# Windowed attention, forward and backward: loading four quads ahead, with one more buffer for x and one less for the turned tokens

## The chip, the cores and the metric

The kernel runs on one core of a Trainium2 chip. The metric is the device time of one execution in microseconds; the figure for a kernel is the median of several runs. One execution of the kernel before was also recorded by the hardware profiler, with every instruction, every semaphore update and every DMA packet. The names used: PE or TensorE (matrix products), DVE or VectorE, ACT or ScalarE, POOL or GpSimd, SP or SyncE, which here only issues DMAs.

## The reference

The input x is an image of 256 x 256 tokens with 384 channels in bfloat16. It is cut into windows of 8 x 8 tokens, attention with one head of 384 channels is computed within each window, and the result is projected. The kernel returns the output and the gradients of x, of `wqkv` and of `wo` for a given gradient of the output.

```python
xw = x cut into 1024 windows of 64 tokens
qkv = xw @ wqkv
q, k, v = (qkv[..., :C], qkv[..., C:2 * C], qkv[..., 2 * C:])
scale = C ** (-0.5)
p = _softmax(jnp.einsum('bqc,bkc->bqk', q, k) * scale, axis=-1)
o = jnp.einsum('bqk,bkc->bqc', p, v) @ wo
_out, _vjp = jax.vjp(_f, x, wqkv, wo)
_grads = _vjp(grad_out)
```

## The kernel before

**Tiling.** Two windows, 128 tokens, fill the 128 partitions; four such pairs make a quad of eight windows. There are 128 quads. Per quad the kernel loads x as the tile `xq` and the gradient of the output as `dq`, each 128 x 4 x 384 in bfloat16, in four DMAs of 96 KB each.

**Weights.** The weights are multiplied together once at the start (`A_sb` from the query and key weights with the scale, `B_sb` from the value weights and `wo`, and their transposes), so that each quad needs fewer products.

**Stages of a quad.** The main loop (L495) runs steps i from 0 to 128, and step i works on three quads at once:

- *quad i+1*: `project` (L173) forms two products with the turned gradient `dT` (kind 0) and the turned x `xT` (kind 1); ScalarE casts them into `yz`, and `gather` (L187) copies them on VectorE into `zy`.
- *quad i*: `scores` (L198), the softmax in six parts (`soft`, L210), and `uv` (L250), whose PSUM banks ScalarE casts into `uq` and `vq`; then `turn` (L260) turns the small probability matrices, on VectorE or, for the first three quads and the last, by a DMA (`crossed`).
- *quad i-1*: `attend` (L283), in four slots: products with `dq`, `xq`, the turned tokens `tok`, `uq` and `vq`; ScalarE and VectorE take the PSUM banks out as `Wq`, `Uq`, `o` and `d`, and GpSimd stores `o` and `d` to memory.

Beside this, each group of `GQ` = 3 finished quads is multiplied into the weight gradients (`gf_rows`, `gf_halves`), two of six products in each step. A quad's `xq` therefore lives until its group is done.

**Turns.** SyncE issues three DMA transposes a quad: `dT` and `xT` from `dq` and `xq` in `load_turn` (L153), called in step i for quad i+2, and `tok` from `zy` in `to_tokens` (L193), called in step i for quad i. `dT` has two buffers, `xT` three, `tok` three.

**Loads.** `load` (L141) is called within step i for quad i + `AHEAD`. It puts four gradient loads on GpSimd's queue (L145), and two x loads on SyncE's (L147); `load_rest` (L149) puts the other two x loads on ScalarE's queue (L151), behind the casts of `yz` and ahead of the casts of `attend`. Ahead of the loop the loads of quads 0, 1 and 2 are issued.

**Order.** Every engine's order is the order of the calls (`manual_schedule`). So SyncE's queue in step i is: `dT` and `xT` of quad i+2, `tok` of quad i, then the two x loads; in the first steps a turn of `cr` into `PS` stands ahead of the x loads. Each engine works its queue in order. The wait of an instruction for its data, for the buffer that it overwrites and for its DMA completion counter is put in by the framework. The counters for DMAs from SyncE and ScalarE are `DMAHW0` to `DMAHW7`, taken in rotation in the order in which the program has the DMAs, and a DMA that takes one waits for the last DMA that used it.

Of the kernel before, what the change touches and what calls it, by code (L numbers as in the profile page):

```python
# [11 lines left out]
BF16 = mybir.dt.bfloat16  # L12
F32 = mybir.dt.float32

P = 128
WIN = 8
WT = WIN * WIN
QUAD = 4
# [5 lines left out]
def kernel(  # L24
# [22 lines left out]
    _, H, W, C = x.shape  # L47
    CK = C // P
# [5 lines left out]
    grp = ctx.enter_context(tc.tile_pool(name="grp", bufs=2 * GQ + 1))  # L54
    qp = ctx.enter_context(tc.tile_pool(name="qp", bufs=2))
# [26 lines left out]
    def fetch_rest():  # L82
        nc.sync.dma_start(out=w_sb[:, :, columns(0)], in_=w_in[:, :, columns(0)])
        nc.scalar.dma_start(out=w_sb[:, :, columns(1)], in_=w_in[:, :, columns(1)])
# [32 lines left out]
    def weight_rest():  # L117
        turn_blocks(B_sb, BT_sb)
        turn_blocks(AT_sb, A_sb)

    def windows(ap, st, first, count=2):
        row, col = st["at"]
        return ap[0, row + WIN * first:row + WIN * (first + count), col:col + WIN, :]
# [2 lines left out]
    OTHER = {0: HI, WT: LO}  # L126

    def load_first(st):
        st["xq"] = xq = grp.tile([P, QUAD, C], BF16, tag="xq", name="xq", bufs=2 * GQ + 4)
        st["dq"] = dq = qp.tile([P, QUAD, C], BF16, tag="dq", name="dq", bufs=6)  # L130
        for t in range(QUAD):
            (nc.sync, nc.scalar)[t % 2].dma_start(out=dq[:, t, :], in_=windows(grad_out, st, 2 * t))
        fetch_rest()
        for t in range(2):
            nc.sync.dma_start(out=xq[:, t, :], in_=windows(x, st, 2 * t))
        nc.gpsimd.tensor_copy(out=spare[:, 0:1], in_=dq[:, QUAD - 1, 0:1])
        for t in range(2, QUAD):
            nc.gpsimd.dma_start(out=xq[:, t, :], in_=windows(x, st, 2 * t))
        nc.gpsimd.tensor_copy(out=spare[:, 1:2], in_=xq[:, 1, 0:1])

    def load(st, on_act=0):  # L141
        st["xq"] = xq = grp.tile([P, QUAD, C], BF16, tag="xq", name="xq", bufs=2 * GQ + 4)
        st["dq"] = dq = qp.tile([P, QUAD, C], BF16, tag="dq", name="dq", bufs=6)
        for t in range(QUAD):
            nc.gpsimd.dma_start(out=dq[:, t, :], in_=windows(grad_out, st, 2 * t))  # L145
        for t in range(QUAD - on_act):
            nc.sync.dma_start(out=xq[:, t, :], in_=windows(x, st, 2 * t))  # L147

    def load_rest(st, on_act):  # L149
        for t in range(QUAD - on_act, QUAD):  # L150
            nc.scalar.dma_start(out=st["xq"][:, t, :], in_=windows(x, st, 2 * t))  # L151
# [39 lines left out]
        nc.vector.tensor_copy(out=st["zy"][:, kind, :, :, :, :], in_=src)  # L191

    def to_tokens(st):  # L193
        st["tok"] = tok = qp.tile([P, 2, CK, QUAD, P], BF16, tag="tok", name="tok", bufs=3)
        nc.sync.dma_start_transpose(out=tok[:].rearrange("p b m t k -> p (b m t) k"),
                                    in_=st["zy"][:].rearrange("p b m t s k -> p (b m t s k)"))

# [177 lines left out]
    def step(c, b, a, ahead):  # L375


        def on(st):
            return (lambda f, *r: f(st, *r)) if st is not None else (lambda f, *r: None)
        C_, B, A = on(c), on(b), on(a)  # L380
        if b is not None and c is None:
            weight_rest()
        B(scores)
        B(soft, 0)
        B(uv, 0, 0)
        B(uv, 0, 1)
        B(soft, 1)
        B(uv, 1, 0)
        B(uv, 1, 1)
        B(soft, 2)  # L390
        B(soft, 3)
        B(uv, 2, 0)
        B(uv, 2, 1)
        B(uv, 3, 0)
        B(uv, 3, 1)
        B(soft, 4)
        for mo in range(CK):
            A(project, 0, mo)
        B(soft, 5)
        B(turn)  # L400
        if ahead is not None:
            load(ahead, ON_ACT)
        A(gather, 0)
        for mo in range(CK):
            A(project, 1, mo)
        if ahead is not None:
            load_rest(ahead, ON_ACT)
        for rows in range(1 if a is not None else 2):
            if fill:
                gf_rows(*fill.pop(0))  # L410
        slots = attention(c) if c is not None else iter(())
        for t in range(QUAD):
            if t == 2:
                A(gather, 1)
            next(slots, None)
        for rest in slots:
            pass
# [4 lines left out]
    quads = [(row, col) for col in range(0, W, WIN) for row in range(0, H, 2 * WIN * QUAD)]  # L422
    n = len(quads)
    sts = [{"at": q, "i": i, "crossed": i < GQ or i == n - 1} for i, q in enumerate(quads)]
    AHEAD = 3
    dw_out = out_2.rearrange("(m p) j -> p m j", p=P)
    dwo_out = out_3.rearrange("(m p) n -> p m n", p=P)

    def weight_gradients(group):
        def product_row(k, out, left, right, sc):  # L430
            pe = ring.tile([P, C], F32, tag="r", name="pe")
            for m in range(CK):
                nc.tensor.matmul(pe[:], lhsT=left[:, m, k * P:(k + 1) * P], rhs=right[:, m, :],  # L433
                                 start=(m == 0), stop=(m == CK - 1))
            if sc is not None and k % 2:
                nc.scalar.activation(out=out, in_=pe[:], func=ACT.Copy, scale=sc)
            elif sc is not None:
                nc.vector.tensor_scalar(out=out, in0=pe[:], scalar1=sc, scalar2=None, op0=ALU.mult)
            else:
                copy_out(k, out, pe[:])  # L440

        def rows(name):
            return grp.tile([P, CK, C], BF16, tag="xq", name=name, bufs=2 * GQ + 4)

        GFT = [grp.tile([P, CK, C], BF16, tag="Wq", name="GFT") for f in range(2)]
        for i in range(CK + 1):
            next(group)
        turn_blocks(GFT[0], final[0])
        for i in range(CK - 1):
            next(group)  # L450
        for part, left, right in ((0, GFT[0], w_sb[:, :, columns(1)]), (1, final[0], w_sb[:, :, columns(0)])):
            dw = rows("dw")
            for k in range(CK):
                product_row(k, dw[:, k, :], left, right, scale)
            nc.sync.dma_start(out=dw_out[:, :, columns(part)], in_=dw[:])
        turn_blocks(GFT[1], final[1])
        dwo = rows("dwo")
        for k in range(CK):
            product_row(k, dwo[:, k, :], w_sb[:, :, columns(2)], final[1], None)
        nc.sync.dma_start(out=dwo_out, in_=dwo[:])  # L460
        dw = rows("dw")
        for k in range(CK):
            product_row(k, dw[:, k, :], GFT[1], woT_sb, None)
            (nc.sync, nc.scalar)[k % 2].dma_start(out=dw_out[:, k, columns(2)], in_=dw[:, k, :])

    with tc.manual_schedule(engines=MANUAL):
        spare = sm.tile([P, 3], BF16, name="spare", bufs=1)
        fetch_weights()
        warm_up(7)
        nc.scalar.copy(out=spare[:, 2:3], in_=B_sb[:, 0, 0:1])  # L470
        make_identity(nc, ident[:])
        nc.gpsimd.memset(GF_acc[:], 0.0)
        load_first(sts[0])
        load(sts[1])
        load(sts[2])
        load_turn(sts[0])
        load_turn(sts[1])
        turn_blocks(wT[2], w_sb, 2 * CK)
        weight_product(BT_sb, wo_sb, wT[2], None)
        turn_on_pe(sts[0], "dq", "dT")  # L480
        for mo in range(CK):
            project(sts[0], 0, mo)
        turn_blocks(wT[0], w_sb, 0)
        turn_blocks(wT[1], w_sb, CK)
        weight_product(A_sb, wT[0], wT[1], scale)
        turn_on_pe(sts[0], "xq", "xT")
        gather(sts[0], 0)
        for mo in range(CK):
            project(sts[0], 1, mo)
        gather(sts[0], 1)  # L490
        turn_on_pe(sts[1], "dq", "dT")
        held = []
        last = None
        get = lambda i: sts[i] if 0 <= i < n else None
        for i in range(n + 1):  # L495
            if 0 <= i < n - 2:
                load_turn(sts[i + 2])
            if 0 <= i < n:
                to_tokens(sts[i])
            step(get(i - 1), get(i), get(i + 1), get(i + AHEAD))  # L500
            if i == 1:
                turn_blocks(woT_sb, wo_sb)
            if i > 0:
                held.append(sts[i - 1])
                sts[i - 1] = None
            if held and i == n:
                last = gf_final(held)
            elif len(held) == GQ:
                fill.extend((held, f, ma) for f in range(2) for ma in range(CK))
                held = []  # L510
        while fill:
            gf_rows(*fill.pop(0))
        weight_gradients(last)
# [30 lines left out]
```

## Time and profile before

| what | value |
|---|---|
| runs | 1904.77, 1904.13 and 1914.19 us |
| median of the runs | 1904.77 us |
| profiled execution, its own time | 1904.35 us |
| its span, first to last instruction | 1902.6 us |
| TensorE clock granted | 1.00 |
| VectorE, ScalarE, GpSimd busy | 88%, 80%, 45% |
| time the packets of SyncE's, GpSimd's and ScalarE's queues took, as shares of 16 DMA engines | 77.8%, 32.0%, 6.2% |
| tok turn, issue to landing | 10.1 us in the median |
| xT turn, issue to landing | 7.6 us |
| dT turn, issue to landing | 7.1 us |
| x load on SyncE and on ScalarE, issue to landing | 4.9 and 6.0 us |
| gradient load on GpSimd, issue to landing | 5.8 us |

How to read it: a line of a group gives the source line, the engine, the operation and the tiles. Lines with SPq or ACTq are DMA issues by the sequencer of SyncE or ScalarE; the time on such a line is that of the issue, and the landing comes later. A wait shown with "<-" names what ended it, as far as semaphore events tell. The shares of the three queues are sums over packets that overlap, so they may add up to more than 100%.

SyncE's queue in time, two steps from the middle of the span (start, length of the issue, what):

```
802.39 1.44 SPq L158 DMA_TRANSPOSE dT<-dq  x1
804.32 3.49 SPq L158 DMA_TRANSPOSE xT<-xq  x1
807.91 5.27 SPq L195 DMA_TRANSPOSE tok<-zy  x1
813.24 1.24 SPq L147 DMA_DIRECT2D xq<-in_x_dram  x2
814.65 2.07 SPq L158 DMA_TRANSPOSE dT<-dq  x1
819.78 1.90 SPq L158 DMA_TRANSPOSE xT<-xq  x1
821.78 4.95 SPq L195 DMA_TRANSPOSE tok<-zy  x1
826.83 1.19 SPq L147 DMA_DIRECT2D xq<-in_x_dram  x2
```

### The profile page before, as it was taken

What the parts mean: (1) busy time and instruction counts of PE and PEld (TensorE: products, weight loads), DVE (VectorE), ACT (ScalarE), POOL (GpSimd) and SP (SyncE); (2) the same over time, 40 slices, a digit from 0 to 9 for tenths busy, and PEclk for the clock granted to TensorE, in tenths of its full rate; (3) what the DMA queues carried; (4) which work ended last, traced back from release to release, by engine and by line L of the source; (5) the groups of instructions that cost most, each with busy time, mean ns of one, the idle gap of its engine ahead of it and who ended that gap; (6) DMA issues with size and microseconds to landing.
All of it is one profiled execution on the core that took longest, in us unless ns stands there. A gap on an engine that the chain in (4) does not pass through costs nothing.

```text
span 1902.6 us, 57253 instructions
## 1 busy us (share of the span) xinstructions
PE 1889.1 (99%) x22333; PEld 1125.4 (59%) x22333; DVE 1668.2 (88%) x3616; ACT 1527.2 (80%) x3354; POOL 859.7 (45%) x1575
## 2 busy tenths in 40 slices
PE   8999999999999999999999999999999999999999
PEld 5565566556655665566556655665565556556655
DVE  5888888888888888888888888888888888888887
ACT  7888878887878788878888887888788878887885
POOL 4444445444444444444444444444444445444432
PEclk9999999999999999999999999999999999999999
DMA  9999999999999999999999999999999999999994
GB/s 206 231 219 227 209 207 226 231 205 222 219 220 216 210 215 228 201 222 223 222 226 198 227 213 220 227 206 216 219 223 225 219 215 215 216 224 221 199 212 104
DMA packets 948913, 408.22 MB, mean 215 GB/s; under 512 B 830689, under 2 KB 924097, under 8 KB 948641
## 3 DMA queue, kind: packets, MB, share of 16 engines
q1 hardware_dynamic: 836224, 228.16, 77.8%
q0 software_dynamic: 75168, 150.91, 32.0%
q10 hardware_dynamic: 37248, 25.48, 6.2%
q8 instruction: 175, 2.87, 0.7%
q14 instruction: 98, 0.79, 0.2%
HBM read 101.84 MB, written 101.84 MB: 107 GB/s over the span
## 4 chain that ended last, share of the span: by engine, by line
PE 96%; DMA 2%; ACT 1%; ACTq 0%; DVE 0%; issue 0%
PE pj L169 51%; PE pg L169 13%; PE ph L353 13%; PE sd L169 5%; PE pw L298 5%; PE po L298 4%; PE pu L298 4%; DMA dT<-dq 2%; PE pd L298 1%; ACTq L151 0%; PE pe L433 0%; ACT yz L185 0%; DMA dq<-in_grad_out_dram 0%; DMA w_sb<-in_wqkv_dram 0%; PE pt L103 0%
## 5 line engine op out<-in xcount | busy, mean ns | idle before, releaser
L318 POOL DMA_DIRECT2D out_dram<-o x512 | 274.0, 535 | 790.7 <-ACT o L302 781.0
L309 ACT CAST Wq<-pw 128x384 bf16<-128x384 f32 x506 | 243.8, 482 | 281.1 <-PE pw L298 270.9
L169 PEld LDWEIGHTS <-xT 128*128 128x128 bf16 x3072 | 291.8, 98 | 182.7 <-issue 0.6
L145 POOL DMA_DIRECT2D dq<-in_grad_out_dram x508 | 268.4, 535 | 184.6 <-PE pj L169 85.6
L169 PE MATMUL pj<-B_sb,xT 128*128 128x384 bf16 x1536 | 333.6, 326 | 0.3 <-issue 0.3
L169 PE MATMUL pj<-AT_sb,xT 128*128 128x384 bf16 x1536 | 333.3, 326 | 0.0
L312 DVE CAST Uq<-pu 128x384 bf16<-128x384 f32 x512 | 282.8, 552 | 16.3 <-PE pu L298 4.1
L320 POOL DMA_DIRECT2D out_dram<-d x480 | 276.6, 576 | 19.9 <-DVE GF_acc L335 5.2
L169 PE MATMUL pj<-xT,A_sb 128*128 128x512 bf16 x1152 | 269.5, 379 | 0.7 <-ACT xT L95 0.7
L169 PE MATMUL pj<-dT,BT_sb 128*128 128x512 bf16 x1152 | 269.5, 379 | 0.6 <-ACT dT L95 0.6
L298 PE MATMUL pd<-tok,ps 64*64 64x384 bf16 x2048 | 256.4, 326 | 3.1 <-ACT o L302 1.7
L183 ACT CAST yz<-pj 128x512 bf16<-128x512 f32 x384 | 225.1, 586 | 38.0 <-PE pj L169 29.3
L302 ACT CAST o<-po 128x384 bf16<-128x384 f32 x512 | 249.6, 488 | 4.4 <-PE po L298 2.7
L258 ACT CAST vq<-pj 128x384 bf16<-128x384 f32 x512 | 247.0, 482 | 3.2
L258 ACT CAST uq<-pj 128x384 bf16<-128x384 f32 x512 | 244.3, 477 | 4.5 <-PE pj L169 2.8
L185 ACT CAST yz<-pj 128x512 bf16<-128x512 f32 x384 | 224.5, 586 | 23.9 <-PE pj L169 0.9
L273 DVE STREAM_TRANSPOSE PS<-ps 32x256 bf16<-32x256 bf16 x496 | 216.2, 436 | 9.5
L169 PEld LDWEIGHTS <-xq 128*128 128x128 bf16 x1572 | 153.6, 98 | 115.2 <-issue 0.9
L353 PEld LDWEIGHTS <-xq 64*64 64x64 bf16 x6000 | 176.3, 107 | 67.3
L353 PE MATMUL ph<-Wq,xq 64*64 64x384 bf16 x3984 | 204.3, 322 | 0.0
L169 PEld LDWEIGHTS <-A_sb 128*128 128x128 bf16 x1152 | 112.7, 98 | 136.4 <-ACT xT L95 0.5
L169 PEld LDWEIGHTS <-BT_sb 128*128 128x128 bf16 x1152 | 112.7, 98 | 122.8 <-DVE dT L97 0.4
(96 smaller groups left out, 3055.4 us busy)
## 6 DMA issues: line engine op xcount, KB each, us to landing
out_dram<-o POOLq DMA_DIRECT2D x512, 96.0 KB, 5.1
dq<-in_grad_out_dram POOLq DMA_DIRECT2D x508, 96.0 KB, 5.8
out_dram<-d POOLq DMA_DIRECT2D x480, 96.0 KB, 5.5
xq<-in_x_dram SPq DMA_DIRECT2D x260, 96.0 KB, 4.9
xq<-in_x_dram ACTq DMA_DIRECT2D x250, 96.0 KB, 6.0
out_dram<-d POOLq DMA_DIRECT2D x64, 48.0 KB, 5.3
tok<-zy SPq DMA_TRANSPOSE x128, 10.1
xT<-xq SPq DMA_TRANSPOSE x127, 7.6
```

The source lines that it names most:

```text
L145: nc.gpsimd.dma_start(out=dq[:, t, :], in_=windows(grad_out, st, 2 * t))
L169: nc.tensor.matmul(out, lhsT=lhsT, rhs=rhs, start=start, stop=stop)
L183: ENG[EV["z"][mo]](out=yz[:, mo, :, 0:4:3, :], in_=pj[:])
L185: ENG[EV["y"][mo]](out=yz[:, mo, :, 1:3, :], in_=pj[:])
L258: cp(out=dst[:, t, :], in_=pj[:])
L298: nc.tensor.matmul(dst[o, :], lhsT=operand(st, lhs, t, h), rhs=operand(st, rhs, t, h), **flags)
L302: copies[EV[name][i]](out=sb[rows, :], in_=src[rows, :])
L309: copies[EV["W"][t] if st["i"] >= GQ else "DA"[t % 2]](out=st["Wq"][:, t, :], in_=pw[:])
L312: copies[EV["U"][t]](out=st["Uq"][:, t, :], in_=pu[:])
L318: nc.gpsimd.dma_start(out=windows(out_0, st, 2 * t), in_=o)
L320: nc.gpsimd.dma_start(out=windows(out_1, st, 2 * t - 1), in_=d if t else above[:])
L353: nc.tensor.matmul(dst[o, :], lhsT=st["xq"][h, t, ma * P + o.start:ma * P + o.stop], rhs=st["UW"[f] + "q"][h, t, :], start=(i == 0), stop= ...
```

## The change

`AHEAD` goes from 3 to 4, so `load` and `load_rest` in step i are for quad i+4. Step 0 gets one call more: `load` of quad 3, with all four of its x loads on SyncE, right behind `tok` of quad 0. The tag `xq` has 11 buffers in place of 10 (3,072 bytes a partition each), and `tok` has two in place of three (6,144 bytes a partition each). `dq` keeps its six buffers.

```diff
@@ load_first, load, rows of weight_gradients
-grp.tile([P, QUAD, C], BF16, tag="xq", name="xq", bufs=2 * GQ + 4)
+grp.tile([P, QUAD, C], BF16, tag="xq", name="xq", bufs=2 * GQ + 5)
@@ to_tokens
-        st["tok"] = tok = qp.tile([P, 2, CK, QUAD, P], BF16, tag="tok", name="tok", bufs=3)
+        st["tok"] = tok = qp.tile([P, 2, CK, QUAD, P], BF16, tag="tok", name="tok", bufs=2)
@@
-    AHEAD = 3
+    AHEAD = 4
@@ the main loop
             if 0 <= i < n:
                 to_tokens(sts[i])
+            if i == 0:
+                load(sts[AHEAD - 1])
             step(get(i - 1), get(i), get(i + 1), get(i + AHEAD))
```

More of the change, by code (lines that the diff above doesn't have):

```diff
@@ L128, in load_first @@
     def load_first(st):
-        st["xq"] = xq = grp.tile([P, QUAD, C], BF16, tag="xq", name="xq", bufs=2 * GQ + 4)
+        st["xq"] = xq = grp.tile([P, QUAD, C], BF16, tag="xq", name="xq", bufs=2 * GQ + 5)
         st["dq"] = dq = qp.tile([P, QUAD, C], BF16, tag="dq", name="dq", bufs=6)
@@ L141, in load @@
     def load(st, on_act=0):
-        st["xq"] = xq = grp.tile([P, QUAD, C], BF16, tag="xq", name="xq", bufs=2 * GQ + 4)
+        st["xq"] = xq = grp.tile([P, QUAD, C], BF16, tag="xq", name="xq", bufs=2 * GQ + 5)
         st["dq"] = dq = qp.tile([P, QUAD, C], BF16, tag="dq", name="dq", bufs=6)
@@ L442, in rows @@
         def rows(name):
-            return grp.tile([P, CK, C], BF16, tag="xq", name=name, bufs=2 * GQ + 4)
+            return grp.tile([P, CK, C], BF16, tag="xq", name=name, bufs=2 * GQ + 5)
         GFT = [grp.tile([P, CK, C], BF16, tag="Wq", name="GFT") for f in range(2)]
```

## The prediction

> **What bounds the kernel now.** I read the page first (engines, slices, queues), then TensorE's waits, then the chain of waits, then SyncE's order in time, and last the waits that the built program holds.
>
> The page and its view of stages, in order. Columns of the third line: stretch, length, then busy time and instructions of PE, PEld, DVE, ACT, POOL; granted clock, share of 16 DMA engines, GB/s.
>
> ```profile
> span 1902.6 us, 57253 instructions
> PE 1889.1 (99%) x22333; PEld 1125.4 (59%) x22333; DVE 1668.2 (88%) x3616; ACT 1527.2 (80%) x3354; POOL 859.7 (45%) x1575
> 69.50:1863.40 1793.90, 1792.22 (x21379) 1069.28 (x21376) 1592.30 (x3443) 1456.38 (x3197) 820.28 (x1500) 1.00 1.19 217
> ```
>
> TensorE is busy in 1792.22 of the 1793.90 us between quad 4's start and the last quad's, at clock 1.00. Modelled ends could hide stalls, so I check the pace in the chain of waits (start, length, what), where one piece marks each quad:
>
> ```profile
> 69.51 7.79 PE pj L169 x42
> 84.08 7.79 PE pj L169 x42
> 98.64 7.79 PE pj L169 x42
> ...
> 521.04 7.79 PE pj L169 x42
> 551.56 7.79 PE pj L169 x42
> 566.12 7.79 PE pj L169 x42
> ```
>
> A quad costs 14.57 us, almost without variation: (521.04 - 69.51) / 31 = 14.566. The step 521.04 to 551.56 is two quads, 29.13, plus 1.39 us of stall. Counted from one step's first score matmul to the next (step i works quad i's scores), just four steps after the start are long: 1.38 (step 36), 1.02 (54, of it 0.34 TensorE's own "issue"), 0.15 (94) and 0.65 us (123): 3.2 us in all. The chain around the first names the cause:
>
> ```profile
> 537.66 7.55 DMA dT<-dq
> 545.21 0.02 issue
> 545.23 0.55 ACTq L151
> 545.78 0.04 issue
> 545.82 1.35 ACTq L151
> 547.17 0.04 issue
> 547.21 0.49 ACT Wq L309
> ```
>
> ScalarE's queue is in order. Its first x load (L151) started 0.02 us after a turn of the gradient landed, and the evictions of the attention stood behind it; TensorE then lacked a PSUM bank (idle 0.98 us). The load does not need that turn. It waits because hardware DMAs (SyncE's and ScalarE's) take completion counters in rotation, eight of them, with seven such DMAs a quad: each waits for the one eight earlier. In the program of before, ScalarE's first load of step i waits for dT of quad i+2. Normally it starts at 8.70 us into the step; wherever it started later than 8.80 us, from step 19 on, that start is dT's landing plus 0.02. A step stalls once the second load's issue ends past about 11.05 us (step 36: end 12.43, stall 1.38).
>
> **The change, part by part.**
>
> *Loads a quad earlier.* Quad 3's second half moves from ScalarE (250 x loads to 248) to SyncE (260 to 262); GpSimd keeps its 508. Nothing is added in sum. What moves is SyncE's waiting. Before:
>
> ```profile
> SPq L158 <- DMA xq<-in_x_dram: 185.3, 146, 3.6
> SPq L158 <- DMA dq<-in_grad_out_dram: 86.2, 51, 5.4
> ```
>
> Those 185.3 + 86.2 us, 2.1 a quad, vanish, as x and gradient landed a step ago. SyncE's medians are 2.1 (dT), 2.5 (xT), 5.7 (tok) and 2 x 0.6 (x), 11.5 us a quad. So the queue can gain some 3 us a quad on TensorE until another wait holds it. TensorE gains nothing from that directly: the least margin from a turn's landing to its first use, from step 5 on, was 9.6 (dT), 6.9 (xT) and 4.5 us (tok).
>
> *One buffer less for tok.* SyncE's tok turn of quad i now waits for the last attention product of quad i-2, which ends about 0.1 us before step i begins (813.79 and 813.89 in the trace). So far it mostly started 4 to 6 us into the step, so that wait is over already unless SyncE gets ahead; then it pins tok at 0 us. Behind it stand the x pair, dT and xT of quad i+3. dT also waits for the projection that frees its old buffer, at 6.7 us. So: tok at 0 to 5.7, x pair to 7, dT to 9.1, xT to 11.7, landing by 17 (7.6 us after issue). They are used over 10 us later, so the new wait costs 0; without that cover a late tok would stop TensorE by its whole delay.
>
> *The counters rotate differently.* In the new program ScalarE's first load waits for **xT** of quad i+2, not dT. At the old phase that would be bad (xT landed at 10.6 us in the median, up to 14.6). At the pinned phase xT lands at about 17 - 14.6 = 2.4 us, 6 us ahead of 8.70. The stalls from late dT go: 1.38 + 0.68 + 0.15 + 0.65 = -2.9 us (bounds -2.9 and 0).
>
> *GpSimd.* Its gradient loads stand at the same place in its queue. The new buffer wait (attention of quad i-2) is met before the output stores ahead of it have gone out: 0.
>
> *The start.* Step 0 now issues four more x loads on SyncE, behind tok of quad 0 (issue ends at 27.84), each 0.6 us; the turn PS of quad 0, first behind them, goes from 27.95 to about 30.4 and lands 3.4 us later, 33.8, before its use at 37.13. But ScalarE's second load of step 0 now waits for the **second** of those four, issued at 28.5. Such a load lands in 4.9 us by the median row; a pair issued at 29.21 landed at 33.5, 4.3 us after its first. So ScalarE is held until 32.8, plus 0.6 for the issue. The next in its queue:
>
> ```profile
> 28.20 0.61 ACTq L151 DMA_DIRECT2D xq<-in_x_dram  x1
> 29.94 0.48 ACT L258 CAST uq<-pj 128x384 bf16<-128x384 f32 x1 [1.40 <-PE pj L169]
> ```
>
> That cast goes from 29.94 to 33.4: 3.4 us late, and TensorE, which soon has no free bank, with it. Bounds: 0 (banks cover it) and 5. I take 3.4, since ScalarE is the busier side there (TensorE waits for its casts at 38.96). Against it: in step 3 ScalarE's second load waited for dT (issued 56.15, 8.83 us to landing), and TensorE idled 1.28 us; dT comes earlier there, -1.3 (bounds -1.9 and 0).
>
> Sum: +3.4 - 2.9 - 1.3 = **-0.8 us**, on the profiled execution's 1904.35 (span 1902.6): 1903.6. The median of the runs lies 0.4 above that execution, so **1904 us**. The bounds give -4.8 to +5.0: 1900 to 1910. About 0.5%, 9.5 us, is what a measurement here tells from no change.
>
> **The rivals.**
>
> *1. Slower: ScalarE's issues beside back-to-back turns.* Pinned, dT and xT go out at 7 to 11.7 in every step, just around the two loads from 8.70. So far these met tok's issue, and the second took 0.55 to 1.51 us. If both take 1.51 the second ends at 8.70 + 1.51 + 0.04 + 1.51 = 11.76, 0.71 past 11.05: 0.71 x 120 = 85 us, 1989. It decides only from an end past 11.05; a tenth of a microsecond past gives 12 us, 1916. For it: the repeated phase. Against: the first took 0.55 even beside tok, and the sum of the longest seen, 8.70 + 0.55 + 0.04 + 1.51, is 10.80. Chance 0.13.
>
> *2. Slower: SyncE does not get ahead.* The queues' packets take 77.8 + 32.0 + 6.2% of 16 engines; if the DMA engines rather than waits set SyncE's pace, xT lands at 10.6 us as before, and ScalarE's first load waits for it: second ends at 10.6 + 0.55 + 0.04 + 0.65 = 11.84, 0.8 us past: 0.8 x 120 = 96 us, 2001. For it: turns took 7 to 10 us to land, 5.6 at best for tok. Against: every stall gives SyncE time that it keeps, so a few quads, some 5 us, should cure it; and tok followed tok within 8.8 us once. Chance 0.08.
>
> The Trainium skill speaks for this rival ("DMA: Bandwidth & Descriptors", Rules for kernel authors): the issuing engines all feed the same 16 DMA engines, so earlier issue buys no bandwidth. That page of the Trainium skill (Latency and other measured facts) has 261 GB/s for a DMA transpose, by which a quad's three turns, 1.57 MB, would need an estimated 6.0 us; by that figure SyncE does get ahead. The trace's 217 GB/s for all traffic does not decide it.
>
> *3. Faster past the bound.* All of TensorE's idle time in the span is 10.05 us, by the first matmul's start and the gaps; 9.5 of it would have to go, though 3.5 of it is before the first step. Chance 0.03.
>
> *4. The change does nothing that counts:* -2.9 fails to come, or the start costs 0; both are inside 1900 to 1910.
>
> **How the numbers follow.** Forecast and 4 together: 0.76 (same). Rivals 1 and 2, 0.21 (slower). Rival 3, 0.03 (faster). The likeliest one's own range is 1900 to 1910; with the near part of rivals 1 and 2 it is 1899 to 1920, leaving out what lies beyond, under 0.2.
>
> **What would show it.** Steps right: SyncE's waits of turns for x and gradient loads gone; tok starting within 1 us of a step's start from about quad 8 on; ScalarE's first load at 8.70 in all steps; steps of 14.57 us with no late ones; ScalarE idle near 28.8 to 32.8 us with the second load of step 0 behind an x landing, and step 1 some 3 us longer. Wrong: loads on ScalarE at 9.6 or later in most steps (by xT's landing: rival 2; by long issues: rival 1), or steps above 14.6 us.

## The result, and the profile after

The changed kernel takes **2033.16 us** in the median of four runs (2015.43 to 2061.71), the kernel before 1905.96 (1904.13 to 1914.19). The ratio is **1.063**, 95% interval 1.054 to 1.072: 6% slower, where no change was forecast. Ratios, here and below, leave out single runs more than 1.5% above the fastest run of their kernel, so a ratio can differ from the quotient of two medians. The profiled execution took 2025.62 us. From its page (span; busy time of each engine; the chain that ended last, by engine and by line; issue to landing of the turns in us):

```profile
span 2023.8 us, 57209 instructions
PE 1934.2 (96%) x22333; PEld 1156.3 (57%) x22333; DVE 1669.6 (82%) x3616; ACT 1531.2 (76%) x3354; POOL 857.6 (42%) x1575
...
PE 72%; DMA 22%; ACTq 2%; ACT 2%; DVE 1%; issue 1%; SPq 1%
...
tok<-zy SPq DMA_TRANSPOSE x128, 11.6
xT<-xq SPq DMA_TRANSPOSE x127, 8.1
```

The instruction counts hardly moved (57253 before). DMAs now hold 22% of the chain (2% before), and TensorE is no longer 99% busy. The turns land later: tok 11.6 us after its issue (10.1 before), xT 8.1 (7.6).

The waits of SyncE's queue (what waits, what ended it: us in all, times, longest):

```profile
SPq L195 <- PE pj L169: 564.4, 89, 7.9
...
SPq L158 <- DMA xq<-in_x_dram: 25.3, 14, 5.0
```

Here the change did what it says: the wait of the turns for x goes from 185.3 us to 25.3. This view counts from the end of SyncE's last issue to the last update of the semaphore before the next issue ends, so it also counts updates that came while an issue was already running; most of the 564.4 us of tok is of that kind. The gaps between SyncE's issues in the trace are plainer. In steps 4 to 122 SyncE stood still for 13.2 us before xT (192.6 in the kernel before), 29.2 before dT (100.6) and 113.9 before tok (13.0). The waits of the other engines show who pays:

```profile
ACT Wq L309 <- issue: 127.9, 25, 7.3
DVE Uq L312 <- PE pu L298: 109.7, 72, 5.8
...
PE pd L298 <- ACT Wq L309: 75.5, 32, 5.1
```

ScalarE stands 127.9 us in front of an eviction (L309) and the profile names no engine for it: what stood there was its own queue's x load. TensorE waits for that eviction. The chain of waits at step 7, which begins at 120.89 us, puts the two together (start, length, what):

```profile
120.96 0.82 PE sd L169 x24
121.78 0.33 SPq L158
122.11 0.05 issue
...
122.21 12.51 DMA xT<-xq
...
134.82 0.55 ACTq L151
...
135.41 0.61 ACTq L151
136.02 0.04 issue
136.06 0.49 ACT Wq L309
...
136.59 0.47 PE pd L298
```

The turn xT of quad 9 is issued at 122.21, lands at the end of that piece, and only then ScalarE's first x load leaves, 13.93 us into the step instead of 8.70. ScalarE's engine has been idle for 5.89 us when it comes to the eviction behind the loads, TensorE idles 3.67 us, and the step takes 19.95 us, 5.38 too many. The idle time is not all of it. At its end the clock granted to TensorE is halved for 3.41 us (stretch, length, then busy time and instructions of PE, PEld, DVE, ACT and POOL; granted clock, share of 16 DMA engines, GB/s):

```profile
120.89:136.00 15.11, 12.03 (x112) 6.73 (x109) 10.75 (x24) 8.76 (x19) 4.34 (x8) 1.00 1.21 176
136.00:139.41 3.41, 2.82 (x36) 2.34 (x39) 1.02 (x2) 2.21 (x6) 2.19 (x4) 0.50 1.20 234
```

In that step TensorE is busy for 16.28 us with the products that take it 14.57 in a step without a stall. In steps 4 to 122 there are 17 such stretches at 0.50, 68.3 us in all. They start in the 17 steps that are longer than 18 us, and in no other; the kernel before has none in these steps.

Over steps 4 to 122 the stalls (step length less 14.567 us) come to 119.7 us in 40 steps (before 2.4 us in 3). In 43 steps the first load starts later than 8.95 us, and those 43 hold 119.3 of the 119.7. In 42 of them its start is xT's landing plus 0.02 us (in step 7 plus 0.10). Of the 119.7 us TensorE is idle for 75.7, practically all of it in front of a product that waits for the eviction of L309; the other 44.0 are longer busy time. By an estimate, half of 68.3, the stretches at half the clock account for at most 34 of those.

Not all steps are like that. Two stretches of the changed kernel's span, steps 5 to 46 and steps 48 to 67 (columns as above):

```profile
91.76:784.95 693.19, 642.05 (x7312) 386.80 (x7309) 544.91 (x1176) 501.04 (x1093) 280.10 (x515) 0.97 1.21 192
799.51:1090.83 291.32, 291.32 (x3485) 173.61 (x3481) 259.11 (x561) 236.69 (x521) 134.38 (x246) 1.00 1.15 218
```

In the second, TensorE is busy the whole time: 291.32 / 20 = 14.57 us a step, at 218 GB/s. In the first it is 693.19 / 42 = 16.50 us, at 192 GB/s. The same program has **two paces**. Up to step 92 it is slow once more, and from 93 to 122 fast. In the fast stretches tok starts 0.06 us before the step, xT lands between 0.6 us before it and 3.5 us into it, and nothing stalls, just as forecast. In the slow one SyncE's queue looks like this (start, length of the issue):

```profile
105.25 3.78 SPq L158 DMA_TRANSPOSE xT<-xq  x1
109.12 7.55 SPq L195 DMA_TRANSPOSE tok<-zy  x1
116.72 1.39 SPq L147 DMA_DIRECT2D xq<-in_x_dram  x2
118.35 3.76 SPq L158 DMA_TRANSPOSE dT<-dq  x1
122.21 6.39 SPq L158 DMA_TRANSPOSE xT<-xq  x1
128.70 7.08 SPq L195 DMA_TRANSPOSE tok<-zy  x1
135.87 1.18 SPq L147 DMA_DIRECT2D xq<-in_x_dram  x2
```

Each issue starts 0.1 to 0.2 us after the last one ended. SyncE stands still for nothing here, and is late. Adding up all its DMA issues per step:

| | SyncE's issues, us a step | step, us | issue of dT, xT, tok (mean) | landing of dT, xT, tok (mean) |
|---|---|---|---|---|
| before, steps 4 to 122 | 11.89 | 14.59 | 2.11, 2.60, 5.97 | 7.12, 7.47, 10.36 |
| after, steps 5 to 46 | **15.95** | 16.50 | 3.22, 4.58, 6.83 | 10.08, 10.34, 12.93 |
| after, steps 48 to 66 | 11.96 | 14.57 | 1.82, 2.94, 5.84 | 6.10, 6.57, 10.83 |

So there are two questions. Why does a late xT stop TensorE at all? And why do the same turns take SyncE 15.95 us in one stretch and 11.96 in the other?

### The profile page after: what moved, and what is told of

Its sections match the earlier page's. It is cut to its first block, busy times and chain, and to the rows that moved or that the text cites. A ratio compares the mean times of both kernels' runs of the same rounds, so it can differ in the third digit from the quotient of the medians.

```text
span 2023.8 us, 57209 instructions
## 1 busy us (share of the span) xinstructions
PE 1934.2 (96%) x22333; PEld 1156.3 (57%) x22333; DVE 1669.6 (82%) x3616; ACT 1531.2 (76%) x3354; POOL 857.6 (42%) x1575
## 4 chain that ended last, share of the span: by engine, by line
PE 72%; DMA 22%; ACTq 2%; ACT 2%; DVE 1%; issue 1%; SPq 1%
PE pj L169 35%; DMA xT<-xq 20%; PE ph L353 11%; PE pg L169 9%; PE sd L169 4%; PE pw L298 4%; PE po L298 3%; PE pu L298 3%; ACTq L151 2%; PE pd L298 2%; DMA xq<-in_x_dram 2%; ACT Wq L309 1%; SPq L158 1%; DMA tok<-zy 0%; PE pe L433 0%
## 5 line engine op out<-in xcount | busy, mean ns | idle before, releaser
L309 ACT CAST Wq<-pw 128x384 bf16<-128x384 f32 x506 | 243.0, 480 | 386.3 <-PE pw L298 227.1
L298 PE MATMUL pd<-tok,ps 64*64 64x384 bf16 x2048 | 281.4, 338 | 76.6 <-ACT Wq L309 75.5
L183 ACT CAST yz<-pj 128x512 bf16<-128x512 f32 x384 | 224.5, 585 | 38.1 <-PE pj L169 29.2
L258 ACT CAST uq<-pj 128x384 bf16<-128x384 f32 x512 | 243.8, 476 | 11.1 <-issue 6.1
L258 ACT CAST vq<-pj 128x384 bf16<-128x384 f32 x512 | 246.6, 482 | 3.5
L353 PEld LDWEIGHTS <-xq 64*64 64x64 bf16 x6000 | 199.0, 111 | 61.9
L353 PE MATMUL ph<-Wq,xq 64*64 64x384 bf16 x3984 | 218.2, 334 | 0.0
L298 PEld LDWEIGHTS <-ps 64*64 64x64 bf16 x3072 | 115.0, 108 | 152.7 <-issue 96.9
L298 PE MATMUL pw<-dq,ps 64*64 64x384 bf16 x1024 | 199.7, 340 | 1.0 <-ACT yz L185 0.7
## 6 DMA issues: line engine op xcount, KB each, us to landing
tok<-zy SPq DMA_TRANSPOSE x128, 11.6
```

Source lines behind the costliest of these rows:

```text
L183: ENG[EV["z"][mo]](out=yz[:, mo, :, 0:4:3, :], in_=pj[:])
L258: cp(out=dst[:, t, :], in_=pj[:])
L298: nc.tensor.matmul(dst[o, :], lhsT=operand(st, lhs, t, h), rhs=operand(st, rhs, t, h), **flags)
L309: copies[EV["W"][t] if st["i"] >= GQ else "DA"[t % 2]](out=st["Wq"][:, t, :], in_=pw[:])
L353: nc.tensor.matmul(dst[o, :], lhsT=st["xq"][h, t, ma * P + o.start:ma * P + o.stop], rhs=st["UW"[f] + "q"][h, t, :], start=(i == 0), stop= ...
```

## The experiments

Theory A answers the first with the counters: ScalarE's first load takes the completion counter that xT had, and waits for it. Theory B says that loads and turns a quad earlier simply crowd the DMA engines, whoever waits. Theory C blames the smaller tok buffer. Theories P and R, formed on the way, are about what SyncE's waits for loads were good for (P) and about the traffic beside the turns (R).

All runs, with the kernel before timed on the same chip each time (ratio to it, 95% interval); stall is that of steps 4 to 122 of the profiled execution, and the last column is for the same steps:

| run | what it is | median us | ratio | stall us | SyncE's issues, us a step |
|---|---|---|---|---|---|
| | before | | 1 | 2.4 | 11.89 |
| | after | 2033.16 | 1.063 [1.054, 1.072] | 119.7 | 14.15 |
| r1 | after, eighth DMA on SyncE | 1926.79 | 1.009 [1.005, 1.013] | 18.8 | 14.11 |
| r2 | after, tok three buffers | 2071.37 | 1.076 [1.068, 1.084] | 170.0 | 15.34 |
| r3 | before, tok two buffers | 1908.44 | 0.999 [0.997, 1.001] | 4.2 | 12.00 |
| r4 | before, eighth DMA on SyncE | 1907.17 | 1.001 [0.998, 1.004] | 1.8 | 12.82 |
| r5 | after, eighth DMA on ScalarE | 1974.19 | 1.031 [1.025, 1.037] | 79.7 | 14.67 |
| r6 | after, all x loads on SyncE | 1909.48 | 1.000 [0.998, 1.002] | 6.7 | 14.01 |
| r7 | after, quad 3 loaded ahead of the loop | 1994.61 | 1.043 [1.037, 1.049] | 98.1 | 13.81 |
| r8 | before, three small DMAs | 2176.96 | 1.139 [1.134, 1.144] | 264.9 | 12.81 |
| r9 | gradient alone four ahead | 1931.09 | 1.010 [1.007, 1.014] | 19.6 | 11.71 |
| r10 | r5 with x alone four ahead | 1939.49 | 1.008 [1.004, 1.011] | 26.5 | 13.86 |
| r11 | r5, short output stores | 1906.86 | 0.999 [0.998, 1.001] | 0 | 9.60 |
| r12 | r6, quad 3 loaded ahead of the loop | 1908.79 | 0.999 [0.997, 1.001] | 7.4 | 14.02 |
| r13 | after, short output stores | 1906.18 | 0.999 [0.997, 1.001] | 1.3 | 9.26 |
| r14 | before, all x loads on SyncE | 1919.76 | 1.002 [0.998, 1.006] | 28.1 | 13.23 |

Two kernels spread widely: r10's ten runs lie between 1911.55 and 1976.45 us and their median is 1.7% above before, r14's between 1907.75 and 1946.36 and 0.6% above. The profiled executions of r2 (2076.55 us) and r5 (1987.90) are among the longer of their four runs.

### The tie: r1 and r4

One small DMA more a step turns the rotation, so that the first load takes its own counter of the step before. r1 does it in the kernel after, r4 in the kernel before, behind the x loads of `load`.

```diff
+        if on_act:
+            nc.sync.dma_start(out=eighth[:, :], in_=windows(x, st, 0)[:, :, 0:32])
...
```

> The changed kernel with one small DMA more on SyncE in each step (128 x 32 elements of x into a tile that nothing reads), so that eight hardware DMAs make a step and each takes the completion counter that it had a step before: ScalarE's first x load then waits for its own landing of the last step, no longer for xT. Theory A (the counter holds ScalarE): the 119.7 us of stall go, 1900 to 1908 us, ScalarE's first load at 8.70 us in nearly every step. Theory B (the earlier loads and turns crowd the DMA engines, and that delays the work itself): still over 1980 us. Theory C (SyncE held by the tok buffer is the cost): still over 1980 us.

> The kernel before with the same small DMA more in each step, so that ScalarE's first load waits for its own landing of the last step and not for dT. Theory A: the 2.9 us of stall in steps 36, 54, 94 and 123 go, 1900 to 1904 us. Theory B: as before or a little slower for the extra traffic, 1904 to 1912 us.

r1 came out at 1.009 instead of 1.063, between what A gave (1900 to 1908) and what B and C gave (over 1980). Only one first load is later than 8.95 us, and the stall falls from 119.7 to 18.8 us. What is left stands behind another wait, in the waits of r1:

```profile
DVE zy L193 <- DMA tok<-zy: 21.2, 12, 4.4
...
PE pd L300 <- DMA tok<-zy: 10.0, 6, 3.1
```

TensorE itself waits for tok. r4 is level with before; its median lies in B's range and not in A's, but the two differ by less than the spread of its runs. Its stall is 1.8 us against 2.4. So the extra DMA is free, and A holds for most of the loss; the remaining 0.9% is not the tie.

### The tok buffer: r2 and r3

```diff
-    ob = ctx.enter_context(tc.tile_pool(name="ob", bufs=8))
+    ob = ctx.enter_context(tc.tile_pool(name="ob", bufs=7))
...
-        st["tok"] = tok = qp.tile([P, 2, CK, QUAD, P], BF16, tag="tok", name="tok", bufs=2)
+        st["tok"] = tok = qp.tile([P, 2, CK, QUAD, P], BF16, tag="tok", name="tok", bufs=3)
```

That is r2, which takes the room for tok from the output tiles; r3 is the edit of tok alone the other way round, in the kernel before.

> The changed kernel with three buffers for tok again; to make room the output tiles o and d have seven buffers in place of eight. ScalarE's first load still waits for xT. Theory A: still slow, 1960 to 2060 us. Theory B: still slow too. Theory C (the third tok buffer was what mattered): 1900 to 1910 us.

> The kernel before with two buffers for tok and nothing else changed: three quads ahead, and ScalarE's first load waits for dT as before. Theory A: as before, 1903 to 1912 us. Theory B: as before. Theory C: over 1950 us.

r3 is level with before, and it has no other edit: C falls, the buffer costs nothing. r2 is as slow as the kernel after or slower (just above A's range); with one buffer less for the outputs it says nothing more exact about tok.

### The tie cut without touching SyncE: r5

In r1 the extra DMA sat in the queue under study. r5 issues it from ScalarE, at the end of the step.

```diff
         for rest in slots:
             pass
+        if ahead is not None:
+            for k in range(1):
+                nc.scalar.dma_start(out=small[k][:, :], in_=windows(x, ahead, 0)[:, :, 0:32])
...
```

> The kernel after, with one more small DMA a step (128 rows of 64 bytes of x into a spare tile) issued by ScalarE at the end of the step, so that a step has eight hardware DMAs; SyncE's queue is as in the kernel after. ScalarE's first x load then takes the counter that it took itself a step earlier, and no longer that of xT. Theory A (the rotation makes ScalarE's first load wait for xT of quad i+2): late first loads (past 8.75 us into the step) by xT's landing gone, stall in steps 4 to 122 under 20 us instead of 119.7, median 1908 to 1928. The eighth DMA on SyncE left 18.8 us of stall with TensorE waiting for tok; if that rest came from the extra issue on SyncE, it is under 6 us here and the median 1908 to 1916. Theory B (loads and turns a quad earlier crowd the DMA engines): median 2000 to 2060 with the stalls behind other waits.

Neither theory's number came. The first x load is in place (8.83 us in the median, later than 8.95 in one step), yet 79.7 us of stall stay. The chain of waits of r5 shows whose:

```profile
1286.94 0.14 PE sd L169 x2
1287.08 16.48 DMA tok<-zy
1303.56 0.04 issue
1303.61 0.53 PE pd L298 x2
```

A tok takes 16.48 us from issue to landing, and TensorE stands 5.85 us for it. SyncE issues for 14.67 us of a mean step of 15.24. The tie was cut and SyncE is still late; A explains how a late turn reaches TensorE, not why it is late. The tie makes TensorE feel xT's landing in the same step, where its own use of xT comes at least 6.9 us after the landing in the kernel before. Why the same small DMA left 0.9% on SyncE and 3.1% on ScalarE is not explained.

### The tie added at three quads ahead: r8

```diff
+        if ahead is not None:
+            for k in range(2):
+                nc.scalar.dma_start(out=small[k][:, :], in_=windows(x, ahead, 0)[:, :, 0:32])
...
+            if 1 <= i < n - 3:
+                nc.sync.dma_start(out=small[2][:, :], in_=windows(x, sts[i], 0)[:, :, 0:32])
```

> The kernel BEFORE (three quads ahead) with three small DMAs more a step (128 rows of 64 bytes each): two by ScalarE at the end of the step, one by SyncE between xT and tok. A step has ten hardware DMAs, and by the rotation ScalarE's first load of step i now waits for xT of quad i+2 instead of dT, as in the kernel after; the second for the small DMA behind that xT. One small DMA a step cost nothing in the kernel before (ratio 1.0008). Theory A: first loads past 8.75 us into the step start at xT's landing plus 0.02 in most steps, stall 30 to 150 us, median 1935 to 2060, though nothing is loaded earlier. Theory B: as before, 1903 to 1915.

It lost 13.9%, but not where expected: hardly any x load starts at xT's landing. The chain of waits of r8:

```profile
304.59 6.79 DMA dT<-dq
311.38 0.02 issue
311.40 0.02 ACTq L420
311.41 0.04 issue
311.45 0.55 ACTq L420
...
312.71 0.49 ACT uq L258
```

The small DMAs themselves (L420) take a turn's counter. In 79 of 125 steps the first of the pair starts within 0.1 us of dT's landing, and the next step's casts (uq, L258) stand behind it, 5.13 us here. Those 79 steps hold 258.7 of the 264.9 us of stall; TensorE is idle for 186.1 us of it, and the rest is longer busy time. As a test of xT's tie the run missed. For the mechanism it speaks plainly: SyncE's issues take 12.81 us a step, so its queue has room, nothing is loaded earlier, and a pair of copies that nobody reads costs nearly all of the loss, because ScalarE issues them and the first took a turn's counter. (The third one, on SyncE, is like the one that was free in r4; it was not tested by itself.)

### No x load on ScalarE: r6 and r14

```diff
-    ON_ACT = 2
+    ON_ACT = 0
```

> The kernel after, with all four x loads of a quad on SyncE, none on ScalarE: no counter can hold ScalarE, and nothing is added to the DMA traffic. SyncE's queue gets two more issues a step, 2 x 0.6 us. Theory A: stalls behind ScalarE gone, stall in steps 4 to 122 under 30 us, what is left behind tok's landing; median 1908 to 1935. Theory B: median 2000 to 2060, since the same loads and turns still crowd the DMA engines.

> The kernel BEFORE (three ahead) with all four x loads of a quad on SyncE, none on ScalarE, as r6 is for the kernel after (1909.48 us). xT on SyncE then waits for x loads that left the same queue a few us ahead of it. If loading a quad earlier is worth something once no counter ties ScalarE to a turn, this kernel is slower than r6: SyncE waits for x in most steps, tok is issued later than 7 us into the step, median 1915 to 1960. If three quads are enough, 1903 to 1912.

r6 loads four quads ahead with the same bytes, and is level with before, as A gave: after one stall of 6.9 us in step 4 there is none. Its landings:

```profile
tok<-zy SPq DMA_TRANSPOSE x128, 7.7
xT<-xq SPq DMA_TRANSPOSE x127, 7.1
dT<-dq SPq DMA_TRANSPOSE x126, 7.7
```

tok lands in 7.7 us (11.6 in the kernel after), though SyncE issues for 14.01 us a step. No x load from ScalarE's queue runs beside tok now; that this is why tok lands sooner was not tested by itself. B as stated falls: the same loads and turns, as early, cost nothing. What is left of B is in the question which queues run beside one another. r14, three quads ahead, has its 28.1 us of stall in steps 4 to 26 and then runs at 14.57 us. It leaves its question open: its median, 1919.76, and a tok issued later than 7 us into the step in 64 of 119 steps are what was said of three quads being too few, but r6 issues tok that late in 52 steps too, and r14's ratio shows no difference to before. r6, with ten runs between 1907.29 and 1914.59, is the steadier.

### Which of the two loads: r9 and r10

r9 loads only the gradient earlier, with the counters as before. r10 is r5 with only x earlier. `load` is split in two for it, `load_g` and `load_x`; the line that differs is shown, with comments added here.

```diff
-            step(get(i - 1), get(i), get(i + 1), get(i + AHEAD))
+            step(get(i - 1), get(i), get(i + 1), get(i + 4), get(i + 3))   # r9: gradient, x
+            step(get(i - 1), get(i), get(i + 1), get(i + 3), get(i + 4))   # r10: gradient, x
```

> The kernel after with only the gradient loaded four quads ahead; x three ahead, with the buffers of x as before (2*GQ + 4) and two of tok. The rotation is that of before: ScalarE's first load waits for dT, and SyncE's xT still waits for the x just loaded; only the wait of dT for the gradient goes. Theory A (counter): as before, 1903 to 1915. Theory P (SyncE's waits for loads had paced the turns; without them they run beside the loads of other queues, take longer, and SyncE's queue falls behind): if the gradient's wait is the pace, SyncE's issue of dT and xT grows from 2.1 and 2.5 us and the median is 1930 to 1980; if x's is, as before.

> The kernel of r5 (four ahead, one small DMA a step on ScalarE, so that no counter ties ScalarE to xT; 1974 us) with only x four quads ahead and the gradient three. SyncE's dT again waits for the gradient of its own step. Theory P with the gradient as the pace: 1903 to 1920, tok's landing 10 to 10.5 us as before (12.1 in r5). Theory P with x as the pace: 1940 to 1990, as r5, tok lands in 12 us and TensorE waits for it. A alone has no reason for r5's 3% and predicts nothing between the two.

r9 is 1.0% slower, at the edge of what P gave for the gradient and outside what A gave, but not by P: the issues of dT and xT stay at 2.1 us in the median. 23 of its first loads come later than 8.95 us, with all of the stall, and they start at dT's landing: the old tie, met oftener. r10 is 0.8% slower by the ratio, with tok landing in 11.0 us and TensorE waiting for it: x without the gradient already brings SyncE from 11.89 to 13.86 us a step, both together to 14.67. P is borne out in part: x's wait is the larger share of the pace, and neither alone makes r5's 3%. Its median, 1939.49, lies just under what was given for x as the pace, and tok lands sooner than the 12 us given there.

### The traffic beside the turns: r11 and r13

r11 is r5, r13 the kernel after itself, with GpSimd's stores cut.

```diff
-        nc.gpsimd.dma_start(out=windows(out_0, st, 2 * t), in_=o)
+        nc.gpsimd.dma_start(out=windows(out_0, st, 2 * t)[:, :, 0:32], in_=o[:, 0:32])
...
-            nc.gpsimd.dma_start(out=windows(out_1, st, 2 * t - 1), in_=d if t else above[:])
+            nc.gpsimd.dma_start(out=windows(out_1, st, 2 * t - 1)[:, :, 0:32], in_=(d if t else above[:])[:, 0:32])
```

> The kernel of r5 with GpSimd's output stores cut to 32 of 384 columns (so most of both large outputs is not written; some 90 of 408 MB less traffic, same instructions). If the turns are slow because other queues' traffic runs beside them, SyncE's issue of dT and xT falls from 2.8 and 3.7 us to 2.2 and 2.6 or less, tok lands in under 10.5 us, no stall is left after the start, 1903 to 1915. If a turn is slow because it follows another turn too closely, they stay and the median stays at 1940 to 1990.

> The kernel after itself (four ahead, seven hardware DMAs a step, so ScalarE's first load still takes xT's counter) with GpSimd's output stores cut to 32 of 384 columns, so most of both large outputs is not written. Theory R (the traffic beside the turns is what keeps SyncE from getting ahead; the counter only carries a late xT to TensorE): tok pinned at 0 us into the step, xT landing before ScalarE's load in every step, no late first loads, stall in steps 4 to 122 under 5 us, median 1903 to 1915. Theory A alone (the counter is enough to make the slow cycle, whatever runs beside): late first loads in a third of the steps or more, stall 60 to 130 us, median 1970 to 2060.

Both are level with before, and r13 still has the tie. Its landings, and its queue in time:

```profile
tok<-zy SPq DMA_TRANSPOSE x128, 8.0
xT<-xq SPq DMA_TRANSPOSE x127, 5.2
dT<-dq SPq DMA_TRANSPOSE x126, 4.1
```

```profile
795.26 2.66 SPq L158 DMA_TRANSPOSE xT<-xq  x1
801.31 3.77 SPq L195 DMA_TRANSPOSE tok<-zy  x1
805.14 2.34 SPq L147 DMA_DIRECT2D xq<-in_x_dram  x2
808.12 1.45 SPq L158 DMA_TRANSPOSE dT<-dq  x1
809.67 1.77 SPq L158 DMA_TRANSPOSE xT<-xq  x1
```

SyncE now has gaps (xT is issued for 2.66 us from 795.26, then nothing until 801.31). tok is pinned 0.06 us before the step, xT lands 0.8 us before it in the median, 9.5 us ahead of ScalarE's load, and all stalls come to 1.3 us. Not one instruction was taken off SyncE; its issues went from 14.15 to 9.26 us a step when some 90 of the 408 MB that all queues move, all of them GpSimd's, no longer ran beside them. R holds: the traffic beside the turns makes SyncE late, and the tie carries it to TensorE. With the traffic the tie costs; without that part of it the tie costs nothing. One other way for the two queues to get in each other's way can be left out: in steps 4 to 122 of the kernel before, 223 x loads of ScalarE were issued inside the issue of a turn on SyncE, and they took 0.55 us in the median, so ScalarE does not wait for SyncE's issue to end.

### The start: r7 and r12

```diff
         load(sts[2])
+        load(sts[3])
...
-            if i == 0:
-                load(sts[AHEAD - 1])
```

> The kernel after, with the loads of quad 3 issued ahead of the loop, right behind those of quad 2, instead of in step 0. The rotation in the loop is that of the kernel after. It asks what the start costs: in the kernel after, step 4 begins 4 to 5 us later than before (TensorE idle 2.39 us at 32.79 while ScalarE's second load waits). If the four loads in step 0 are that cost, step 4 begins within 1 us of the kernel before (68.6 us) and the rest stays: stall in steps 4 to 122 of 90 to 150 us, median 2000 to 2060. Theory A and B both expect the slow pace to stay; a pace as before (under 1920) would say that the start sets whether SyncE gets ahead.

> The kernel of r6 (four ahead, all x loads on SyncE; 1909.48 us, with 6.9 us of stall in step 4 and none after) with quad 3's loads issued ahead of the loop. If the four loads in step 0 made that stall, it goes: step 5 starts under 88 us instead of 93.2 and the median is 1901 to 1906, at most 0.4% below r6 and level with before. Otherwise 1907 to 1912.

r12 is the edit of r6 and that of r7 together. In r7 step 1 takes 14.04 us, as short as before (14.42; 18.50 in the kernel after): the four loads in step 0 are that cost. But step 3 takes 15.43 us, and step 4 begins at 69.80, 1.2 us after before's 68.64. The slow pace stays, with a median just under the range given. In r12 the second of the two cases came: step 4 is still 22.12 us long and step 5 begins at 92.06, so r6's early stall does not come from those four loads. No version here is shown to be faster than before, and with TensorE at 14.57 us in nearly all steps there was little to win.

## Why the prediction was wrong

**What bounds the kernel: right.** TensorE at 14.57 us a quad is the floor of both kernels, and of r6, r11 and r13.

**SyncE's waits for loads go: right,** 185.3 + 86.2 us to 25.3 + 5.1 in the view of waits, and the gaps say the same. **"So the queue can gain some 3 us a quad on TensorE until another wait holds it": wrong, and this is the step that failed.** It subtracted SyncE's issues (2.1 + 2.5 + 5.7 + 1.2 = 11.5 us) from the step and took them for fixed. They had been read in a kernel in which SyncE's own waits for x and gradient held dT and xT back until those loads had landed. Without the waits the same issues take 15.95 us in the slow stretch, 1.4 more than a step of 14.57 has, so SyncE falls back instead of getting ahead. What its issues take depends on the traffic beside them: 9.26 us a step with short stores (r13) and 14.15 with whole ones, in kernels that are otherwise the same. Why it is 15.95 in one stretch of the kernel after and 11.96 in another stays open.

**Rival 2** was that case: DMA engines setting SyncE's pace, ScalarE's first load at xT's landing, TensorE without a bank. It gave 96 us; the stalls measure 119.7, not as 0.8 us in every step but as some 3 us in each of 40, and 44.0 of them are longer busy time of TensorE, which the prediction has nowhere. That the two totals are near is luck. What spoke against it, "every stall gives SyncE time that it keeps, so a few quads, some 5 us, should cure it", was the same mistake: a stall gives time once, and the deficit is there again in the next steps. The cure did come, in step 47, after 85.3 us of stalls, and it did not last: in steps 68 and 69 tok took 7.04 and 8.79 us to issue, and the slow pace was back.

The Trainium skill's rule cited there ("DMA: Bandwidth & Descriptors", Rules for kernel authors) is that spreading DMAs over the issuing engines doesn't help bandwidth, since all run on the same 16 DMA engines; that issuing earlier buys none either is the prediction's own conclusion. The trace does not contradict it, with 192 GB/s in the slow stretch and 217 before, but the same bytes over longer steps would show that in any case. Its 261 GB/s for a DMA transpose, an estimated 6.0 us for a quad's turns, was reached in no run: the least mean sum of their three issues is 7.7 us (r13), and there a tok alone takes 8.0 us from issue to landing.

**One buffer less for tok costs 0: right** (r3: 0.999; more buffers, r2, do not help). **tok pinned, xT at about 2.4 us into the step: right wherever the fast pace holds**, steps 48 to 67 and 93 to 122, and in nearly all of r13, where xT lands earlier still; wrong in the others.

**The counters: the mechanism right, the cover wrong.** "At the old phase that would be bad" is what happened in steps 5 to 46. No load of ScalarE waits for dT any more, so the stalls behind the -2.9 us went, but in the slow stretches those behind xT took their place. Where SyncE is ahead nothing is left: no stall in steps 48 to 67, 1.3 us in all of r13.

**GpSimd: 0** was not tested by itself.

**The start, +3.4:** step 1 grew by 4.1 us (18.50 against 14.42), with TensorE idle for 2.39 at 32.79. That the four loads do it is right (r7), and the size is a little low, but another tie held ScalarE first. Its first load of step 0 started at 33.13, 0.02 us after tok of quad 0 had landed, whose counter it took; the second left at 33.74, when the landing that the prediction named (33.46) was past. **Step 3, -1.3: wrong.** The idle of 1.28 us is still there, and step 3 takes 13.84 us against 13.83.

**Rival 1** (long issues on ScalarE beside the turns) did not happen: where xT was early, the first load started at 8.70, and next to nothing stalled.

## What to carry to other kernels

The length of a DMA issue on a queue is not a constant of the instruction: measure how much it shrinks or grows with the traffic beside it before counting on slack in that queue, and ask what a wait that you remove had been keeping apart. List which earlier DMA each DMA's completion counter belonged to, also across queues; an edit that only reorders DMAs can tie an engine that computes to a transfer that it has nothing to do with. If an engine with evictions to do issues loads, moving those loads to a queue that only issues DMAs removes the tie, and here it cost nothing, with 14.01 us of issues in a step of 14.6 (r6). A stall of TensorE can cost more than its idle time: look at the granted clock behind it.

## What the runs showed that was not expected

**Two paces of one program.** Steps 5 to 46 of the kernel after take 16.50 us and steps 48 to 67 take 14.57, with the same instructions. The switch goes both ways, and its trigger is not settled; r7 and r14 have it too. In the slow pace the turns' packets of 256 bytes take 31 ns in the mean and 85 ns at the 95th percentile, in the fast one (steps 48 to 66) 26 and 42; GpSimd's packets of 4,608 bytes take 349 and 965 ns against 290 and 581. That fits with what the Trainium skill says of one DMA engine that has work from several queues ("DMA: Bandwidth & Descriptors", Queues, rings and completion order): it serves them in turn, a whole packet at a time; a packet there is a run of descriptors, and need not be what the profile counts as one. By that a small packet can stand behind a large one. That this is how the issues grow is argued, not shown; shown is that they shrink when the stores do.

**A DMA's issue can be paid for by whoever stands behind it.** In r8 copies of 8 KB on ScalarE, two a step, go with 258.7 of 264.9 us of stall while the DMA engines moved only 189 GB/s (215 before).
